# Loading q and k as long runs, in a softcap attention fused with a bilinear feed-forward layer

## The chip, the core and the metric

The kernel runs on one core of a Trainium2 chip. Time is device time of one launch in microseconds (us). The engines are TensorE (PE, with its weight loads as PEld), VectorE (DVE), ScalarE (ACT), GpSimd (POOL) and SyncE (SP); SP, ACT and POOL have queues from which they issue DMAs.

## The reference, cut to what matters

```python
# q, k, v: (4, 12, 448, 64) float32, cap a scalar; w_a, w_b: (768, 1536), w_out: (1536, 768), float64
scores = np.matmul(q, k.transpose(0, 1, 3, 2)) / np.sqrt(64)
scores = cap * np.tanh(scores / cap)
attn = softmax(scores)                       # over the keys, 1e-9 added to the sum
x = np.matmul(attn, v)                       # heads side by side: (1792, 768)
out = (x @ w_a) * (x @ w_b) @ w_out          # (1792, 768) float32
```

The weights come as 64-bit floats and are made into 32-bit floats on the chip, by integer operations on the two halves of each word (`load64`, `conv`).

## The kernel before, in words

**Pairs.** The 48 heads are worked through as 24 pairs. Pair `pi` has head `hp` on partitions 0 to 63 and head `hp + 6` on partitions 64 to 127. For each pair q and k are loaded (`load_k`), transposed to "feature by position" in 32 x 32 blocks on DVE (`turn`), and multiplied on PE (`scores`, four pieces `c`: three of 128 keys for both heads, one of the last 64). ACT makes tanh of each piece and exp of each half (`tanh`, `exp`); PE multiplies by v (`attend`, two halves); DVE adds the probabilities up and PE sums them (`add_full`, `add_last`, `sums_last`, `sums`). The reciprocal of the sums goes to DRAM and comes back spread over 64 partitions as `den` (`store_rec`, `load_den`); DVE scales (`scale`) and splits x into two parts, `xhi` and `xlo` (`split_x`).

**Two half batches.** Pairs 0 to 11 are the first half batch, and their x stays in SBUF. Pairs 12 to 23 are interleaved with the feed-forward layer of the first half (`hidden`, `gate`, `project`, `collect`), and their x is stored in DRAM for the second. `hidden(g, f, nm, h)` covers columns of x for batch `h` of the half: `h = 1` reads x of pairs 6 to 11. Each feed-forward product is made of three products of high and low parts.

**How q and k are loaded (lines 204 to 220).** One transfer `n` fills 32 partitions: `n` is a head of the pair and a half of its 64 features. It takes 32 features of each key, 128 bytes, so a head is 448 packets. Pairs 0 and 1 are loaded head by head, k from SP and q from ACT; pairs 2 to 11 two pairs at a time, from SP, into the accumulator `acc`, which nothing else uses yet; pairs 12 to 23 into one buffer for k and one for q (`ld`).

**The order of the work.** The order on every engine is written out once, when the program is built. PE's order is fixed by hand (`scores_of`, `attend_of`, `sums_of`, and `ffn(us)`, which puts in about `us` of feed-forward pieces). For the rest a planner (lines 513 to 848) gives each job an engine, a cost in us, a lag until its result can be used, and what it needs; due times run back from PE's order. It simulates the engines and, whenever one is free, picks the startable job that is due first. `MOVE` is a transfer's time in this model. Every engine then executes its list strictly in order. The order of SP's queue therefore also decides what a transfer waits behind.

**The start.** `warm_up` (lines 741 to 755) clears constants on DVE and runs dummy matmuls on PE. `load_cap` is issued by ACT after q of pair 0; `limits` computes six values from it on DVE, one exp on ACT, two more values on DVE, before the first tanh.

Of the kernel before, what the change touches and what calls it, by code (L numbers as in the profile page):

```python
# [119 lines left out]
def kernel(  # L120
# [75 lines left out]
    own, krem = (slice(0, D), slice(D, P)), (S - R, 0)  # L196
# [5 lines left out]
    early_rows = acc.rearrange("p t d -> p (t d)")  # L202

    def load_k(pi, nm, n, heads):
        b, hp = divmod(pi, NP)
        src = k if nm == "k" else q
        j, h = divmod(n, D // BLK)
        if pi < NPG:
            at = (NP * (nm == "q") + hp) * S
            if n == 0:  # L210
                for i in range(heads):
                    raw[nm, pi + i] = early_rows[:, at + i * S : at + (i + 1) * S]
            to = early_rows[n * BLK : (n + 1) * BLK, at : at + heads * S]
        else:
            if n == 0:
                raw[nm, pi] = ld.tile([P, S], F32, tag=f"ld{nm}", name=f"ld{nm}_{pi}")
            to = raw[nm, pi][n * BLK : (n + 1) * BLK]
        rows = src[b, j * NP + hp : j * NP + hp + heads].rearrange("m s d -> (m s) d")
        eng = nc.scalar if nm == "q" and pi < 2 else nc.sync
        eng.dma_start(to.rearrange("p (c d) -> p c d", d=BLK), rows[:, h * BLK : (h + 1) * BLK].rearrange("(c p) d -> p c d", p=BLK))  # L220

    def load_v(pi, n):
        b, hp = divmod(pi, NP)
        t = vb[pi % 3]
        j = n % 2
        src = v[b, hp + j * NP]
        eng = nc.gpsimd if 3 <= pi < NPG else nc.sync
        if n < 2:
            rows = src[j * R : j * R + NC3 * P].rearrange("(c p) d -> p c d", p=P)
            eng.dma_start(t[:, j * (NC3 + 2) : j * (NC3 + 2) + NC3], rows)  # L230
        else:
            eng.dma_start(t[own[j], NC3 + j], src[krem[j] : krem[j] + R])
# [18 lines left out]
    def last_keys(pi):  # L251
        for z, x in zip(kz, stk["k", pi]):
            for j, o in enumerate(own):
                nc.scalar.copy(z[o, j * R : (j + 1) * R], x[o, krem[j] : krem[j] + R])
# [3 lines left out]
    def scores(pi, c):  # L258
        tk, tq = stk["k", pi], stk["q", pi]
        psc = ps_sc.tile([P, 2, 512], F32, tag="pssc", name=f"psc_{pi}_{c}")  # L260
        full = c < NC3
        if pi < NPG:
            for j, o in enumerate(own):
                at = j * R + c * P if full else krem[j]
                to = psc[:, j, :S] if full else psc[o, 0, :S]
                nc.tensor.matmul(to, tk[o, at : at + (P if full else R)], tq[o], start=True, stop=True)  # L266
        elif full:
            for x, y in products:
                for j, o in enumerate(own):
                    kk = tk[x][o, j * R + c * P : j * R + (c + 1) * P]  # L270
# [253 lines left out]
    def loads(pi, heads):  # L524
        pairs = range(pi, pi + heads)
        for nm in "kq":
            eng = "ACT" if nm == "q" and pi < 2 else "SP"
            for n in range(P // BLK):
                free = [("turn", nm, p - NP) for p in pairs] if pi < NPG else [("turn", nm, pi - 1)]
                needs = [("load", nm, pi, n - 1)] if n else free  # L530
                job(("load", nm, pi, n), eng, 0.52, load_k, (pi, nm, n, heads), needs, 3.2 if pi < 2 else 4.0)
                jobs["load", nm, pi, n].order_only = n > 0
                for p in pairs:
                    jobs["load", nm, p, n] = jobs["load", nm, pi, n]
        for p in pairs:
            for n in range(4):
                eng, us = ("POOL", 0.7) if 3 <= p < NPG else ("SP", 0.52)
                needs = [("load", "v", p, n - 1)] if n else [("attend", p - 3, 1)]
                job(("load", "v", p, n), eng, us, load_v, (p, n), needs, 4.0)
                jobs["load", "v", p, n].order_only = n > 0  # L540
# [29 lines left out]
    def turns(pi):  # L570
        for nm in "kq":
            free = [("scores", pi - 2, c) for c in range(SUB)] + [("lo", nm, pi - 1)]
            job(("turn", nm, pi), "DVE", 0.56, turn, (pi, nm), [*(("load", nm, pi, n) for n in range(P // BLK)), *free])
# [21 lines left out]
    def attend_of(pi):  # L595
        for hf in range(2):
            on_pe(("attend", pi, hf), 1.52, attend, (pi, hf), [("exp", pi, hf), *evac.get(pv_bank(pi), ()), *(("load", "v", pi, n) for n in range(4))])
        if pi in ON_PE:
# [7 lines left out]
    def ffn_piece(key):  # L606
# [21 lines left out]
        else:  # L628
# [8 lines left out]
            if f == NF // GF - 1:  # L637
                if (g, x) == (NG - 1, NTI - 1) or h:
                    job(("out", g, x, h), "SP", 0.5, store_out, (g, x, h), [("collect", g, f, x, 0), ("collect", g, f, x, h)])
# [19 lines left out]
    SOON, RAW, BACKLOG = 4.0, 24.0, 3.0  # L659
# [3 lines left out]
    for pi, heads in ((0, 1), (1, 1), *((i, 2) for i in range(2, NPG, 2)), *((i, 1) for i in range(NPG, NPAIR))):  # L663
        loads(pi, heads)
# [3 lines left out]
    for pi in range(NPG):  # L668
        for c in (0, 1):
            scores_of(pi, c)  # L670
        if pi:
            attend_of(pi - 1)
# [13 lines left out]
    for pi in range(NPG, NPAIR + 1):  # L686
# [5 lines left out]
        if pi < NPAIR:  # L692
# [5 lines left out]
            ffn(GAP / 2 if pi > NPG else 7.2)  # L698
# [13 lines left out]
    for t, (nm, f, g) in enumerate(seq):  # L712
        if g == 0:
            parts = 6 if t < 4 else 2
            for n in range(parts):
                needs = [("raw", t, n - 1)] if n else [("conv", t - 2, 5)]
                job(("raw", t, n), "POOL" if t < 6 else "SP", 0.8 if t < 6 else 0.5, load64, (t, n, parts), needs, 4.0, RAW + 6.0 * (t + n / parts) if t < 4 else 0.0)
                jobs["raw", t, n].order_only = n > 0
            steps = (("ACT", 0.82), ("ACT", 0.8), ("DVE", 0.48), ("DVE", 0.48), ("DVE", 0.88), ("POOL", 2.1))
            for n, (eng, us) in enumerate(steps):  # L720
# [3 lines left out]
                job(("conv", t, n), eng, us, conv, (t, n), needs, 0.5)  # L724
# [15 lines left out]

    def warm_up():
# [7 lines left out]
        nc.vector.memset(sel, 0.0)  # L749
        for z in kz:  # L750
            nc.vector.memset(f32(z), 0.0)
        nc.vector.memset(sel[:, Q - QS : Q], 1.0)
        nc.vector.memset(both, 0.0)
        for j, o in enumerate(own):
            nc.vector.memset(both[o, Q + (j - 1) * QS : Q + j * QS], 1.0)

    def limits():
# [5 lines left out]
        nc.vector.tensor_scalar_mul(capt[:, 1:2], capt[:, 6:7], 1.0 / math.sqrt(D))  # L763
        nc.scalar.activation(capt[:, 7:8], capt[:, 0:1], AF.Exp, scale=-1.0)
# [3 lines left out]
    def load_cap():  # L768
        nc.scalar.dma_start(capt[:, 3:4], cap.rearrange("(a b) -> a b", b=1).to_broadcast([P, 1]))

    job("cap", "ACT", 0.5, load_cap, (), [("load", "q", 0, 3)], 2.4)
    jobs["cap"].order_only = True
    job("limits", "DVE", 1.3, limits, (), [("turn", "q", 0), "cap"])
    jobs["tanh", 0, 0].needs.append("limits")

# [35 lines left out]
    order, port, moved = [], 0.0, 0.0  # L811
    MOVE = {load_k: 0.46, load_v: 0.5, load64: 1.7, store_rec: 0.15, load_den: 0.4, store_w: 1.0, reload_w: 1.0, store_x: 0.57, reload_x: 0.65, store_out: 1.0}
    def starts(x):
# [3 lines left out]
        if x.move and x.fn not in (store_rec, load_den):  # L817
            t = max(t, moved - BACKLOG)
        return t

    for x in real:
        x.move = MOVE.get(x.fn, 0.0) * (x.args[3] if x.fn is load_k else 0.2 if x.fn is load_v and x.args[1] > 1 else 2 / x.args[2] if x.fn is load64 else 1.0)
        x.shared = x.eng == "DVE" and x.fn not in (turn, recip, scale, collect) and not (x.fn is gate and x.args[3] == 0)
    while len(order) < len(real):
# [12 lines left out]
        if x.move:  # L837
            moved = max(moved, t + 1.3) + x.move
            x.end = max(x.end, moved + 0.7)
# [54 lines left out]
```

## Time and profile before

| | us |
|---|---|
| median of 3 runs | 717.72 (717.03 to 718.0) |
| the profiled execution | 718.51 |
| its span | 716.7 |
| PE busy | 703.4 |
| DVE busy | 423.0 |
| ACT busy | 347.7 |
| POOL busy | 112.0 |

The span runs from the first to the last instruction; the execution's own time has 1.8 us around it. PE's busy time contains the dummy matmuls of the start. In rows of the trace "idle before" is the time that an engine stood still ahead of an instruction, and the arrow names what ended it. Times in rows count from the span's start.

### The profile page before, as it was taken

What the parts mean: (1) busy time and instruction counts of PE and PEld (TensorE: products, weight loads), DVE (VectorE), ACT (ScalarE), POOL (GpSimd) and SP (SyncE); (2) the same over time, 40 slices, a digit from 0 to 9 for tenths busy, and PEclk for the clock granted to TensorE, in tenths of its full rate; (3) what the DMA queues carried; (4) which work ended last, traced back from release to release, by engine and by line L of the source; (5) the groups of instructions that cost most, each with busy time, mean ns of one, the idle gap of its engine ahead of it and who ended that gap; (6) DMA issues with size and microseconds to landing.
All of it is one profiled execution on the core that took longest, in us unless ns stands there. A gap on an engine that the chain in (4) does not pass through costs nothing.

```text
span 716.7 us, 11238 instructions
## 1 busy us (share of the span) xinstructions
PE 703.4 (98%) x4370; PEld 578.3 (81%) x4370; DVE 423.0 (59%) x649; ACT 347.7 (49%) x474; POOL 112.0 (16%) x104
## 2 busy tenths in 40 slices
PE   7999998999999999999999999999999999999996
PEld 2333356879879789779879779999999999999996
DVE  4678897676679688686974849432043424434232
ACT  5989986577777566575646630222321112202100
POOL 0536431231322222222221100000000000000000
PEclk9999999999999999999999999999999999999999
DMA  9999585758777857858646437331022013101013
GB/s 128 152 171 170 140 212 123 193 143 200 184 170 193 193 141 177 201 138 227 157 116 159 146 101 248 110 109 45 11 83 83 23 34 99 53 15 44 1 45 113
DMA packets 142739, 90.55 MB, mean 126 GB/s; under 512 B 108024, under 2 KB 128536, under 8 KB 142680
## 3 DMA queue, kind: packets, MB, share of 16 engines
q1 hardware_dynamic: 135784, 82.53, 46.8%
q0 software_dynamic: 3040, 6.79, 4.0%
q10 hardware_dynamic: 3856, 0.46, 0.5%
q8 instruction: 36, 0.59, 0.4%
q14 instruction: 23, 0.19, 0.1%
HBM read 67.24 MB, written 22.50 MB: 125 GB/s over the span
## 4 chain that ended last, share of the span: by engine, by line
PE 92%; DMA 3%; SPq 2%; DVE 1%; ACT 1%; issue 0%; ACTq 0%; DVEq 0%
PE pv L308 10%; PE po L493 8%; PE po L494 8%; PE po L495 8%; PE phb L460 8%; PE phb L462 8%; PE phb L461 8%; PE pha L460 8%; PE pha L462 8%; PE pha L461 8%; PE psc L266 5%; PE psc L271 3%; DMA den<-rd 2%; PE pv L329 2%; SPq L220 1%; PE psc L274 1%
## 5 line engine op out<-in xcount | busy, mean ns | idle before, releaser
L493 PE MATMUL po<-who,gh 128*128 128x384 f32 x336 | 113.4, 337 | 0.0
L495 PE MATMUL po<-who,gl 128*128 128x384 f32 x336 | 112.5, 335 | 0.0
L494 PE MATMUL po<-wlo,gh 128*128 128x384 f32 x336 | 112.5, 335 | 0.0
L460 PE MATMUL pha<-xhi,wha 128*128 128x448 f32 x288 | 105.0, 365 | 2.7 <-DVE xhi L374 2.7
L460 PE MATMUL phb<-xhi,whb 128*128 128x448 f32 x288 | 105.2, 365 | 0.0
L462 PE MATMUL pha<-xhi,wla 128*128 128x448 f32 x288 | 104.8, 364 | 0.0
L461 PE MATMUL pha<-xlo,wha 128*128 128x448 f32 x288 | 104.6, 363 | 0.2 <-DVE xlo L375 0.2
L462 PE MATMUL phb<-xhi,wlb 128*128 128x448 f32 x288 | 104.6, 363 | 0.0
L461 PE MATMUL phb<-xlo,whb 128*128 128x448 f32 x288 | 104.3, 362 | 0.0
L283 ACT ACTIVATE pf<-psc,capt 128x896 f32<-128x896 f32 (+1 forms) x96 | 84.3, 909 | 29.6 <-PE psc L271 19.3
L308 PE MATMUL pv<-pf,vb 128*64 128x448 f32 x384 | 78.8, 553 | 0.0
L287 ACT ACTIVATE pf<-pf,capt 128x1792 f32<-128x1792 f32 (+1 forms) x48 | 77.1, 1606 | 0.8
L504 DVE TENSOR_TENSOR acc<-po,acc 128x384 f32<-128x384 f32 x84 | 46.4, 553 | 43.0 <-PE po L495 42.9
L467 ACT COPY asb<-pha 128x448 f32<-128x448 f32 x48 | 25.4, 531 | 81.8 <-PE pha L462 81.0
L493 PEld LDWEIGHTS po<-who,gh 128*128 128x128 f32 x336 | 63.1, 188 | 2.4 <-issue 1.2
L494 PEld LDWEIGHTS po<-wlo,gh 128*128 128x128 f32 x336 | 63.1, 188 | 0.1
L495 PEld LDWEIGHTS po<-who,gl 128*128 128x128 f32 x336 | 63.1, 188 | 0.0
L308 PEld LDWEIGHTS pv<-pf,vb 128*64 128x64 f32 x384 | 25.8, 139 | 45.5 <-issue 38.0
L477 DVE TENSOR_TENSOR asb<-phb,asb 128x448 f32<-128x448 f32 x48 | 29.9, 622 | 53.4 <-PE phb L462 53.4
L460 PEld LDWEIGHTS pha<-xhi,wha 128*128 128x128 f32 x288 | 54.0, 187 | 8.8 <-DVE xhi L374 3.4
L460 PEld LDWEIGHTS phb<-xhi,whb 128*128 128x128 f32 x288 | 54.0, 187 | 6.4 <-issue 2.5
L479 ACT CAST gh<-asb 128x448 fp32r<-128x448 f32 x48 | 27.2, 566 | 66.0 <-DVE asb L477 65.6
(103 smaller groups left out, 1038.4 us busy)
## 6 DMA issues: line engine op xcount, KB each, us to landing
w64o<-in_moe_w_out_dram SPq DMA_DIRECT2D x24, 384.0 KB
w64a<-in_moe_w_a_dram SPq DMA_DIRECT2D x18, 384.0 KB
w64b<-in_moe_w_b_dram SPq DMA_DIRECT2D x18, 384.0 KB
den<-rd SPq DMA_DIRECT2D x48, 112.0 KB
out_dram<-acc SPq DMA_DIRECT2D x13, 384.0 KB
wda<-wta SPq DMA_DIRECT2D x12, 384.0 KB
wdb<-wtb SPq DMA_DIRECT2D x12, 384.0 KB
wdo<-wto SPq DMA_DIRECT2D x12, 384.0 KB
```

The costliest lines, as they stand in the source:

```text
L266: nc.tensor.matmul(to, tk[o, at : at + (P if full else R)], tq[o], start=True, stop=True)
L283: nc.scalar.activation(to, prob.pop((pi, "s", c))[:, :n, :S], AF.Tanh, scale=capt[:, 1:2])
L287: nc.scalar.activation(pf, pf, AF.Exp, scale=capt[:, 0:1])
L308: nc.tensor.matmul(t[o, :S], tv[:, j * (NC3 + 1) + (c if j == 0 else (c + 1) % (NC3 + 1))], p, start=(c == 0), stop=(c == NC3))
L460: nc.tensor.matmul(t[:, :S], wh[:, kk], xhi[:, kk, cs], start=(kk == 0), stop=False)
L461: nc.tensor.matmul(t[:, :S], wh[:, kk], xlo[:, kk, cs], start=False, stop=False)
L462: nc.tensor.matmul(t[:, :S], wl[:, kk], xhi[:, kk, cs], start=False, stop=(kk == NK - 1))
L477: nc.vector.tensor_mul(t, phs.pop(("b", h))[:, :S], t)
L493: nc.tensor.matmul(t[:, :HALF], gh[:, cs], wh, start=(f == fs[0]), stop=False)
L494: nc.tensor.matmul(t[:, :HALF], gh[:, cs], wl, start=False, stop=False)
L495: nc.tensor.matmul(t[:, :HALF], gl[:, cs], wh, start=False, stop=(f == fs[-1]))
L504: nc.vector.tensor_add(acc[:, ti, hs], t, acc[:, ti, hs])
```

## The change

A transfer of q or k now takes, for each of 32 partitions, one run of consecutive memory: partition p gets keys 14 p to 14 p + 13, all 64 features of each but the last 32 of the last key (or the first 32 of the first). So each of the two transfers of a head brings also the features that it doesn't use, and 14 x 64 numbers a partition are kept where 14 x 32 are read. The transpose reads blocks of 32 features and writes with a stride of 14 elements, so that keys come out in their order. The remaining 64 keys (`rest`) are now the last ones for both heads, before they were the first ones for the second head.

With this go: each pair is loaded by itself (before, pairs 2 to 11 came two at a time); six slots in `acc` instead of twelve, so a load waits for the transpose of three pairs before; from pair 12 on one buffer for k and q together; pair 0 is loaded in turn from SP and ACT. Cap is loaded by POOL at the very start; `limits` is cut in two, and only the first part stands before the first tanh. Memsets move from DVE to POOL; the dummy matmuls are nine of 128 columns. Raw weights 4 and 5 move from POOL's queue to SP's. On PE the first half of `attend(0)` goes ahead of the scores of pair 1, and after the scores of pair 12 only 3.6 us of feed-forward are put in instead of 7.2. The planner's costs change, and it lets no more than 8 transfers be under way.

```diff
     def load_k(pi, nm, n):
...
-        rows = src[b, j * NP + hp : j * NP + hp + heads].rearrange("m s d -> (m s) d")
-        eng = nc.scalar if nm == "q" and pi < 2 else nc.sync
-        eng.dma_start(to.rearrange("p (c d) -> p c d", d=BLK), rows[:, h * BLK : (h + 1) * BLK].rearrange("(c p) d -> p c d", p=BLK))
+                at = (2 * pi + (nm == "q")) % EARLY * RUN
+                raw[nm, pi] = rows_of[:, at : at + RUN]
+            else:
+                raw[nm, pi] = ld.tile([P, RUN], F32, tag="ld", name=f"ld{nm}_{pi}")
+        width = RUN - D + BLK
+        eng = nc.scalar if pi == 0 and n % 2 else nc.sync
+        runs = src.rearrange("(p c) d -> p (c d)", p=BLK)
+        eng.dma_start(raw[nm, pi][n * BLK : (n + 1) * BLK, :width], runs[:, h * BLK : h * BLK + width])
...
     def turn(pi, nm):
-        t = raw.pop((nm, pi))
+        t = raw.pop((nm, pi)).rearrange("p (c d) -> p c d", d=D)[:, :, :BLK]
         tt = qk.tile([P, S], F32, tag=f"t{nm}", name=f"t{nm}_{pi}")
-        nc.vector.transpose(tt, t)
         stk[nm, pi] = tt
+        nc.vector.transpose(tt.rearrange("p (d c) -> p c d", d=BLK), t)
...
-        eng = nc.gpsimd if t < 6 else nc.sync
+        eng = nc.gpsimd if t < 4 else nc.sync
...
+            free = [("turn", nm, pi - EARLY // 2)] if pi < NPG else [("turn", "q", pi - 1)] if nm == "k" else [("turn", "k", pi)]
...
+        if pi == 1:
+            attend_of(0, (0,))
...
-            ffn(GAP / 2 if pi > NPG else 7.2)
+            ffn(GAP / 2 if pi > NPG else 3.6)
...
     def warm_up():
+        load_cap()
         warm = bank(0, "warm")
-        nc.vector.memset(psum[0][:, 0], 0.0)
-        for n in (S, S, S, S // 2):
-            nc.tensor.matmul(warm[:, :n], psum[0][:, 0, :P], psum[0][:, 0, :n], start=True, stop=True)
+        nc.vector.memset(psum[0][:, 0, :P], 0.0)
+        for n in range(9):
+            nc.tensor.matmul(warm[:, :P], psum[0][:, 0, :P], psum[0][:, 0, :P], start=True, stop=True)
...
+    job("limits", "DVE", 1.0, limits, (), (), None, 4.0)
+    job("floors", "DVE", 0.4, floors, (), ["limits"])
+    for c in range(2):
+        jobs["tanh", 0, c].needs.append("floors" if c else "limits")
```

## Rows read from the trace of the kernel before

**Rows 1.** The page, part 1: busy time, share and instructions by engine.
```profile
PE 703.4 (98%) x4370; PEld 578.3 (81%) x4370; DVE 423.0 (59%) x649; ACT 347.7 (49%) x474; POOL 112.0 (16%) x104
```

**Rows 2.** Table by stretch, PE alone: stretch, length, busy, clock, DMA share, GB/s.
```profile
0.00:20.00 20.00, 15.92 (x58) 1.00 0.96 132
...
80.00:130.00 50.00, 47.04 (x418) 0.97 0.68 150
...
440.00:716.70 276.70, 270.77 (x1430) 1.00 0.20 64
```

**Rows 3.** Instructions in order of time, 0 to 30 us: start, duration, instruction.
```profile
0.75 4.32 SPq L220 DMA_DIRECT2D acc<-in_k_dram  x7
...
1.40 5.05 PE L745 MATMUL warm<-psum 128*128 128x448 f32 x8 [1.40 <-DVE psum L743]
...
6.11 0.65 DVE L237 STREAM_TRANSPOSE tq<-acc 128x448 f32<-128x448 f32 x1 [3.11 <-DMA capt<-in_cap_dram]
...
7.14 1.28 ACT L764 ACT_TABLE_LOAD   x1 [7.14 <-DMA acc<-in_q_dram]
...
7.33 1.77 PE L266 MATMUL psc<-tq,tk 64*128 64x448 f32 x8 [0.89 <-DVE capt L758]
...
7.99 0.15 DVE L763 TENSOR_SCALAR capt<-capt 128x1 f32<-128x1 f32 x1
...
8.54 1.89 ACT L283 ACTIVATE pf<-psc,capt 128x896 f32<-128x896 f32 x2
...
12.82 1.92 PE L266 MATMUL psc<-tq,tk 64*128 64x448 f32 x8 [1.32 <-ACT pf L283]
```

**Rows 4.** Chain of waits, 0 to 20 us: start, duration, what.
```profile
12.25 0.53 ACT pf L283
```

**Rows 5.** Chain of waits, 80 to 130 us.
```profile
95.37 2.25 DMA den<-rd
...
109.24 0.42 SPq L220
...
112.90 5.98 DMA den<-rd
...
121.62 0.60 PE pha L461
```

**Rows 6.** Waits of PE: us in total, times, longest.
```profile
PE pha L460 <- DVE xhi L374: 2.7, 1, 2.7
```

**Rows 7.** Table by stretch, PE alone, after the wait at 118.
```profile
120.96:127.60 6.64, 6.45 (x49) 0.74 0.23 37
```

**Rows 8.** DMA view, 0 to 2 us (rate in 40 slices) and 2 to 4 us.
```profile
GB/s 0 0 0 0 0 0 0 0 0 0 0 0 0 0 0 0 0 0 0 0 0 0 0 0 0 0 0 0 0 0 0 0 0 0 0 10 72 84 105 95
...
DMA packets 2848, 0.35 MB, mean 176 GB/s; under 512 B 2848, under 2 KB 2848, under 8 KB 2848
```

**Rows 9.** Table by stretch, all engines; the last two columns are DMA share and GB/s.
```profile
500.00:600.00 100.00, 100.00 (x531) 96.13 (x530) 32.00 (x47) 22.47 (x38) 0.00 (x0) 1.00 0.17 52
```

**Rows 10.** Groups of DVE instructions: shapes, count, busy us, mean ns, idle before.
```profile
L417 DVE SCALAR_TENSOR_TENSOR wta<-w64a,wta 128x768 int32<-128x768 int32 x12 | 11.3, 946 | 0.2
...
L237 DVE STREAM_TRANSPOSE tk<-ldk 128x448 f32<-128x448 f32 x12 | 7.6, 635 | 0.1
```

**Rows 11.** The page, part 6: DMA issues, KB each, median us to landing.
```profile
vb<-in_v_dram POOLq DMA_DIRECT2D x18, 16.0 KB, 3.7
```

**Rows 12.** Instructions in order of time, ACT and DVE, 95 to 130 us.
```profile
113.07 1.43 ACT L287 ACTIVATE pf<-pf,capt 128x1344 f32<-128x1344 f32 x1
...
119.52 1.08 DVE L294 TENSOR_TENSOR psum<-psum,pf 128x896 f32<-128x896 f32 x1
```

**Rows 13.** Table by stretch: busy PE, PEld, DVE, ACT, POOL; clock, DMA share, GB/s.
```profile
80.00:110.00 30.00, 29.91 (x313) 16.47 (x312) 27.42 (x46) 27.01 (x34) 9.63 (x12) 1.00 0.74 170
200.00:300.00 100.00, 100.00 (x638) 83.56 (x637) 77.95 (x109) 65.49 (x94) 23.14 (x12) 1.00 0.73 181
```

**Rows 14.** Waits of SP's DMA queue: us in total, times, longest.
```profile
SPq L220 <- DVE tk L237: 43.6, 9, 7.2
```

More of the change, by code (lines that the diff above doesn't have):

```diff
@@ L194, with load_k @@
     vb = [const.tile([P, 2 * NC3 + 2, D], F32, tag=f"vb{i}", name=f"vb{i}") for i in range(3)]
-    own, krem = (slice(0, D), slice(D, P)), (S - R, 0)
+    own, rest = (slice(0, D), slice(D, P)), slice(S - R, S)
     raw, stk, prob, pvs = {}, {}, {}, {}
     ON_PE = set(range(3, NPG))
-    early_rows = acc.rearrange("p t d -> p (t d)")
-    def load_k(pi, nm, n, heads):
+    rows_of = acc.rearrange("p t d -> p (t d)")
+    RUN = S * D // BLK
+    EARLY = NTI * DM // RUN
+    def load_k(pi, nm, n):
         b, hp = divmod(pi, NP)
-        src = k if nm == "k" else q
         j, h = divmod(n, D // BLK)
[L208 to L217, printed above, removed]
-        rows = src[b, j * NP + hp : j * NP + hp + heads].rearrange("m s d -> (m s) d")
-        eng = nc.scalar if nm == "q" and pi < 2 else nc.sync
-        eng.dma_start(to.rearrange("p (c d) -> p c d", d=BLK), rows[:, h * BLK : (h + 1) * BLK].rearrange("(c p) d -> p c d", p=BLK))
+        src = (k if nm == "k" else q)[b, j * NP + hp]
+        if (nm, pi) not in raw:
+            if pi < NPG:
+                at = (2 * pi + (nm == "q")) % EARLY * RUN
[6 more added lines that the diff above has]
+        eng.dma_start(raw[nm, pi][n * BLK : (n + 1) * BLK, :width], runs[:, h * BLK : h * BLK + width])
     def load_v(pi, n):
@@ L263, in scores @@
             for j, o in enumerate(own):
-                at = j * R + c * P if full else krem[j]
                 to = psc[:, j, :S] if full else psc[o, 0, :S]
-                nc.tensor.matmul(to, tk[o, at : at + (P if full else R)], tq[o], start=True, stop=True)
+                kk = tk[o, c * P : (c + 1) * P] if full else tk[o, rest]
+                nc.tensor.matmul(to, kk, tq[o], start=True, stop=True)
         elif full:
@@ L522, in job, with loads @@
         jobs[key] = Piece(eng, us, LAG[eng] if lag is None else lag, list(needs), fn, args, after)
-    def loads(pi, heads):
-        pairs = range(pi, pi + heads)
+    def loads(pi):
         for nm in "kq":
-            eng = "ACT" if nm == "q" and pi < 2 else "SP"
+            free = [("turn", nm, pi - EARLY // 2)] if pi < NPG else [("turn", "q", pi - 1)] if nm == "k" else [("turn", "k", pi)]
             for n in range(P // BLK):
[L529 to L540, printed above, removed]
+                needs = free if n == 0 or pi == 0 else [("load", nm, pi, n - 1)]
+                job(("load", nm, pi, n), "ACT" if pi == 0 and n % 2 else "SP", 0.52, load_k, (pi, nm, n), needs, 3.0 if pi < 2 else 4.0)
+                jobs["load", nm, pi, n].order_only = n > 0 and pi > 0
+        for n in range(4):
+            eng, us = ("POOL", 0.7) if 3 <= pi < NPG else ("SP", 0.52)
+            needs = [("load", "v", pi, n - 1)] if n else [("attend", pi - 3, 1)]
+            job(("load", "v", pi, n), eng, us, load_v, (pi, n), needs, 4.0)
+            jobs["load", "v", pi, n].order_only = n > 0
     def softmax(pi):
@@ L572, in turns @@
             free = [("scores", pi - 2, c) for c in range(SUB)] + [("lo", nm, pi - 1)]
-            job(("turn", nm, pi), "DVE", 0.56, turn, (pi, nm), [*(("load", nm, pi, n) for n in range(P // BLK)), *free])
+            free += [("load", nm, pi, n) for n in range(P // BLK)]
+            job(("turn", nm, pi), "DVE", 0.56, turn, (pi, nm), free)
             if pi >= NPG:
@@ L593, in scores_of, with attend_of @@
         slots.append(("tanh", pi, c))
[L595 to L598, printed above, removed]
+    def attend_of(pi, halves=(0, 1)):
+        for hf in halves:
+            on_pe(("attend", pi, hf), 1.52, attend, (pi, hf), [("exp", pi, hf), *(() if hf else evac.get(pv_bank(pi), ())), *(("load", "v", pi, n) for n in range(4))])
+        if pi in ON_PE and 1 in halves:
             on_pe(("sums_last", pi), 0.35, sums_last, (pi,))
@@ L658 @@
     CYCLE, turns_of = ((0, 1, 2), (3, 1, 2, 0)), [3, 3, 1, 2, None]
-    SOON, RAW, BACKLOG = 4.0, 24.0, 3.0
+    SOON, RAW, BACKLOG, DEPTH = 4.0, 24.0, 3.0, 8
     HASTY = (gate, keep_a, collect, recip, store_rec, load_den, scale)
     GAP = 20.4
-    for pi, heads in ((0, 1), (1, 1), *((i, 2) for i in range(2, NPG, 2)), *((i, 1) for i in range(NPG, NPAIR))):
-        loads(pi, heads)
+    for pi in range(NPAIR):
+        loads(pi)
     for pi in range(NPAIR):
@@ L671 @@
         if pi:
-            attend_of(pi - 1)
+            attend_of(pi - 1, (0, 1) if pi > 1 else (1,))
         for c in (3, 2):
@@ L716 @@
                 needs = [("raw", t, n - 1)] if n else [("conv", t - 2, 5)]
-                job(("raw", t, n), "POOL" if t < 6 else "SP", 0.8 if t < 6 else 0.5, load64, (t, n, parts), needs, 4.0, RAW + 6.0 * (t + n / parts) if t < 4 else 0.0)
+                job(("raw", t, n), "POOL" if t < 4 else "SP", 0.8 if t < 4 else 0.5, load64, (t, n, parts), needs, 4.0, RAW + 6.0 * (t + n / parts) if t < 4 else 0.0)
                 jobs["raw", t, n].order_only = n > 0
@@ L723 @@
                     needs += [("lo", t - AHEAD), ("keepw", t - AHEAD), ("full", t - 1)]
-                job(("conv", t, n), eng, us, conv, (t, n), needs, 0.5)
+                job(("conv", t, n), eng, us, conv, (t, n), needs, 1.5 if eng == "POOL" else 0.5)
             job(("keepw", t), "SP", 0.52, store_w, (t,), [("conv", t, 5)], 3.0)
@@ L818, in starts @@
             t = max(t, moved - BACKLOG)
+        if x.move and x.eng != "POOL" and len(landed) >= DEPTH:
+            t = max(t, landed[-DEPTH])
         return t
     for x in real:
-        x.move = MOVE.get(x.fn, 0.0) * (x.args[3] if x.fn is load_k else 0.2 if x.fn is load_v and x.args[1] > 1 else 2 / x.args[2] if x.fn is load64 else 1.0)
-        x.shared = x.eng == "DVE" and x.fn not in (turn, recip, scale, collect) and not (x.fn is gate and x.args[3] == 0)
+        x.move = MOVE.get(x.fn, 0.0) * (0.2 if x.fn is load_v and x.args[1] > 1 else 2 / x.args[2] if x.fn is load64 else 1.0)
+        x.shared = x.eng == "DVE" and x.fn not in (turn, limits, floors, recip, scale, collect) and not (x.fn is gate and x.args[3] == 0)
     while len(order) < len(real):
@@ L838 @@
             moved = max(moved, t + 1.3) + x.move
-            x.end = max(x.end, moved + 0.7)
+            x.end = max(x.end, moved + (1.7 if x.fn is load64 else 0.7))
+            if x.eng != "POOL":
+                landed.append(t + x.us + 1.7 if moved < t + 1.6 + x.move else moved + 0.4)
         free[e] = t + x.us
```

33 lines of the change are left out of this document (15 added, 18 removed).

## The prediction

> **What bounds the kernel now.** I read the page first. TensorE (PE) is busy 703.4 of 716.7 us, and that is 98% of the span [rows 1]. So the whole kernel is a line of matmuls, and a change can win only where that line has holes. The table by stretch says where they are [rows 2]: 4.1 us in the first 20 us, 3.0 between 80 and 130, and the 5.9 of the last stretch, most of them the tail after the last matmul, which nothing here touches; of the 13.3 that the span has in all, 0.3 are left for everything else. The first 20 us hide more than 4.1, because 5.05 us of their busy time is the warm-up loop, which computes nothing [rows 3].
>
> Then I read both holes closely. At the start [rows 3]: q and k of pair 0 are transposed from 6.11 to 7.27, scores start at 7.33, the first tanh at 8.54, the first exp ends at 12.25, and from 12.82 PE runs without a hole of a microsecond. Up to there it does two rows of scores, 1.77 + 1.92 = 3.7 us of work. The chain of waits says what is late [rows 4]: ACT (ScalarE) is on it from 7.14, first with the table load, which stands behind ACT's own nine DMA issues [rows 3], then with tanh and exp up to 12.78.
>
> The second hole is the join of attention and feed-forward, at 118. The hidden piece with h = 1 needs x of pair 11. Its denominator was issued at 112.90 and took 5.98 us to land; scale, add and split follow, PE goes on with x's high part at 120.96 and with the low part at 121.62 [rows 5]. PE waits 2.7 us there [rows 6], and pays again: from 120.96 to 127.60 the granted clock averages 0.74, so part of that stretch ran at the lower level (1.2 GHz) after the wait. That is 0.26 x 6.64 = 1.7 us [rows 7]. The hole costs 4.4 us.
>
> **The change, part by part.**
>
> *Loads of q and k.* One transfer was 448 packets of 128 B (56 KB); it becomes 32 runs of 3456 B (108 KB), half of it thrown away. Between 2 and 4 us small packets moved at 176 GB/s with the engines full [rows 8]. Later, with rows of 3 KB, 52 GB/s were moved at a busy share of 0.17, so 306 at full share [rows 9]. Pair 0 is 8 transfers: 0.46 MB / 176 = 2.6 us before, 0.88 MB / 306 = 2.9 us after. So the bytes take no less time; the gain is in the order: all eight are now issued first, four from SP and four from ACT, while before three of k of pair 1 were already on their way by 5.07 and shared the engines [rows 3]. First bytes flow at 1.8 (the slices of that view are 0.05 us), 1.8 + 2.9 = 4.7, plus half a microsecond for v's transfers issued behind them: q is there at about 5.2, k before it. If the new runs went only at the 176 of the small ones, 5.0 us, it would be 7.3; that is the bad end.
>
> *Transpose.* 48 of them at some 635 ns for 448 elements a partition [rows 10]. Its write now has a stride of 56 B. No row shows such a write; the nearest is conv, which reads 768 elements at a stride of 8 B in 946 ns, 1.23 ns an element against the 1.42 of the transpose [rows 10]. By that row: no cost. The other bound is twice the time, +0.62 us each; gain I exclude, the elements are the same. I take 0.
>
> The Trainium skill (SBUF — State Buffer, section Door 1) says that SBUF is read and written in 16-byte lines and that a pattern that leaves its line with every access pays for it; 56 B does. No run here shows it; by it the transposes slow, which is the second rival below.
>
> *Cap first, limits split.* Cap goes from ACT's queue to GpSimd's (POOL) ahead of everything. A small POOL transfer lands 3.7 us after issue [rows 11], so at some 4.3; six small VectorE (DVE) operations (from 7.20, the last from 7.99 [rows 3]) then end by 5.2, before q's transpose. ACT has four issues instead of nine, so its table load (1.28 us, from 7.14 before) runs before 5. Scores can start at 5.2 + 0.65 (transpose, k's is done) + 0.1 = 5.95. The first scores take about 0.9 of the 1.77, so tanh starts near 6.95 instead of 8.54.
>
> *First half of attend(0) ahead of scores of pair 1.* Before, PE waited for the third tanh (12.78, that is 4.24 after the first); now it can start attend(0, 0) when exp ends, 3.71 after the first tanh [rows 3, 4]. PE's unbroken work begins at 6.95 + 3.75 = 10.70 instead of 12.82, with the same 3.7 us done before it: **-2.1 us**. Behind it, scores of pair 1 want their loads by 12: 16 issues from SP (pair 0 four, v four, pair 1 eight) at some 0.5 us (0.42 and the gap behind it [rows 5]) end by 9.5 and land by 11.7. That is covered, by half a microsecond.
>
> *Warm-up.* 9 x 128 = 1152 columns instead of 1568: 5.05 x 0.73 = 3.7 us from about 1.1, so it ends at 4.8 and the gap to scores is 1.15 (0.89 before). A gap of 1.32 before 12.82 left the granted clock at 1.00 [rows 2, 3]. I take no cost; were the clock low, the first scores cost some 0.9 us more. Bounds for the start as a whole: -3.2 (q at 4.2) to +0.6 (176 GB/s).
>
> *More issues.* Pairs 2 to 11 had 40 double transfers, now 80: +40 x 0.5 = 20 us of SP between 10 and 80, or 2 us per pair of 7.6 us (scores 2 x 1.9, attend 3.2, sums 0.6); the 8 issues take 4.2, with rec, den and weights some 6.5 in all. That is hidden by PE, which is the bound there. The rest of a pair (v, den) is unchanged, and the transfers have 3 pairs (23 us) ahead of need instead of 6. Raw weights 4 and 5 move from POOL to SP: 4 issues, 2 us, hidden likewise.
>
> *The join.* In place of 7.2 us of hidden pieces after the scores of pair 12 only 3.6 are put there, so attend(12) (3.2), sums (0.6) and the first scores of pair 13 (1.4) come ahead of the piece that waited. That moves its need of x of pair 11 from 118.1 to 123.3; x was ready at 121.6, so 1.7 us to spare without any faster DMA. Besides, between rec's store and the issue of den six loads of k and q were issued, 3.1 us, and their small packets lay ahead of den [rows 5]; a den on a quiet queue took 2.25. attend(12) wants its exp, which ended at 114.5 against 114.9: just there [rows 12]. So the hole goes with its clock loss: **-4.4 us** (bounds: 0, if another wait stands there, to -4.6).
>
> After 130 PE has no hole, DVE and ACT are busy 0.78 and 0.65 of 200 to 300 [rows 13], and the k and q pair has one shared buffer for 28 us of work per pair. I cost it at nothing; the cover is that slack.
>
> Sum on the profiled execution: 718.51 - 2.1 - 4.4 = **712.0 us**. The median of the runs shown is 0.8 lower than that execution; I leave 712.0, as the start term has more below it than above.
>
> **Rivals.**
>
> *The wait changes its place.* sums(12) needs the second add of pair 12. Before, it stood on DVE behind the scale that waited for den, and ended at 120.6 [rows 12]. If the written order keeps it there, PE waits at 118.1 for up to 2.5 us and loses the clock again (1.7): the join gives 0.3 to 1. For it: DVE is 0.91 busy from 80 to 110 [rows 13], and POOL, SP and DVE are all re-ordered by the planner. Against: sums is due earlier now, and the planner sorts by that. 718.5 - 2.1 - 0.5 = 715.9.
>
> *The stride is paid.* +0.62 us per transpose. At the start +0.6. From 80 to 110 six transposes, 3.7 us, meet 2.6 us of idle DVE [rows 13], so 1.1 to 3.7 late, say 2.4: 718.5 - 1.5 - 4.4 + 2.4 = 715.0. Elsewhere DVE has room.
>
> *Slower: the one buffer holds up SP.* From pair 12 on, q's load waits for k's transpose, and the next k's for q's; SP issues in order, so den, rec and the weights stand behind. SP already waits for tk 43.6 us, 4.8 each time [rows 14]. If two such waits stand ahead of rec and den of pair 11, x is 9.7 late, 8.0 beyond the 1.7 to spare; with the clock 9.7: 718.5 - 6.5 + 9.7 = 721.7. It turns to slower from 6.5 us of such waits (1.7 to spare and 1.7 of clock cancel out). Against: only k and q of pairs 12 to 14 fall before the join.
>
> *No gain at the start* (transfers at 176 GB/s) together with a moved wait: 718.5 + 0.1 - 0.5 = 718.1.
>
> **How the numbers follow.** Forecast 0.50, moved wait 0.20, stride paid 0.12, SP held up 0.12, nothing gained 0.06. A measurement of this kernel tells about 0.2% from no change, that is 716.3 and 719.2. Faster: 0.50 + 0.12 + 0.14 of the moved wait = 0.76. Same: 0.06 of it + 0.05 = 0.11. Slower: 0.13. The range 709.0 to 717.0 holds the first three (start at -3.2 and some of the 20 to 80 holes below, a moved wait at its worst above) and leaves out 0.18.
>
> **What would show it.** In the trace after: scores from about 6, first tanh near 7, PE without holes from about 10.7; attend(12) directly after the third hidden piece, no hole before the x split, granted clock 1.00 from 110 to 130; transposes at 0.62 us; 128-byte packets of q and k gone, about 6000 long ones in their place. Wrong if: transposes take 1.2 us; SP shows waits on tk or tq ahead of den; PE waits at sums(12) or scores of pair 13; ACT or DVE are late for the weights between 85 and 110 now that PE comes 2 us sooner.

## The result, and the profile after

The change makes the kernel slower: 728.23 us (four runs, 726.93 to 729.52) against 717.86 (717.03 to 719.6) in the same job, a ratio of 1.0141 with a 95% interval of 1.0113 to 1.0169. The profiled execution of after took 728.93 us with a span of 727.2; that is 10.5 more than the span of before.

The page of after, part 1 (busy us, share of the span, instructions), answers to [rows 1].

```profile
PE 707.0 (97%) x4380; PEld 580.5 (80%) x4380; DVE 436.0 (60%) x642; ACT 348.0 (48%) x474; POOL 110.2 (15%) x108
```

PE is busy 3.6 us longer with slightly less to compute and idle 6.9 us longer (20.2 against 13.3). The table of PE by stretch says where; it answers to [rows 2] (stretch, its length, PE busy, granted clock, DMA share, GB/s).

```profile
0.00:20.00 20.00, 14.99 (x58) 1.00 0.80 185
20.00:80.00 60.00, 57.69 (x508) 1.00 1.00 219
80.00:130.00 50.00, 44.77 (x385) 0.93 0.75 190
440.00:727.20 287.20, 281.50 (x1491) 0.99 0.22 70
```

Between 20 and 80 the DMA engines are full (share 1.00), and the large hole is new: it stands just before 83, where before had none. The last stretch idles 5.7 us, as before. PE's own list of waits (total, times, longest) answers to [rows 6].

```profile
PE psc L265 <- DVE capt L769: 3.6, 1, 3.6
PE pv L307 <- DVE den L357: 3.5, 1, 3.5
PE pv L307 <- ACT w64b L405: 2.2, 1, 2.2
PE pv L328 <- DVE psum L293: 1.8, 1, 1.8
```

The work is the same in both kernels, so I lay the two traces side by side by a landmark: the sums of a pair, 28 matmuls of 128x64. Sums of pair 0 start at 29.19 (26.82 before), so **the start costs 2.4 us**. Sums of pair 7 start at 91.26 (80.20 before); at sums of pairs 9 and 10 the difference is 10.9 (106.88 against 95.96). So 8.5 us come **behind the start**: 2 of them in small steps (1.6 between the sums at 51.93 and at 61.18) and 6.5 at the hole, between the sums at 77.13 and at 91.26. At the end it is 10.5: **the join gives back less than half a microsecond**.

*The start.* The timeline of after from 0 to 30, all engines (start, length, engine, line, operation, count, idle time before and what ended it), answers to [rows 3].

```profile
1.27 0.68 POOL L739 DMA_DIRECT2D capt<-in_cap_dram  x1 [0.80 <-POOLq L880]
...
5.94 0.15 DVE L759 TENSOR_SCALAR capt<-capt 128x1 f32<-128x1 f32 x1 [3.92 <-DMA capt<-in_cap_dram]
...
6.95 0.94 DVE L237 STREAM_TRANSPOSE tk<-acc 128x448 f32<-128x448 f32 x1
...
7.90 0.94 DVE L237 STREAM_TRANSPOSE tq<-acc 128x448 f32<-128x448 f32 x1
...
8.90 5.97 PE L265 MATMUL psc<-tq,tk 64*128 64x448 f32 x16 [3.62 <-DVE capt L769]
...
29.19 0.65 PE L328 MATMUL pv<-psum,sel 128*32 128x64 f32 x28
```

Cap lands 4.6 us after POOL's issue, at 5.9, and the six limits (5.94 to 6.95) now stand on DVE ahead of both transposes. q lands at 7.7, by the chain of waits (start, length, what):

```profile
2.16 5.55 DMA acc<-in_q_dram
```

So scores start at 8.90 instead of the 5.95 that I forecast, after 3.6 us in which PE does nothing. Sixteen instructions of scores then take 5.97 us, where before two rows of eight took 1.77 and 1.92 [rows 3]. The granted clock of 1.00 in the table is no reading here: the trace of after has no record of that clock before 13.77 us, and a stretch without a record counts as 1.00. The kernel with upper and lower partitions in turn (below) starts in nearly the same way and has records: after a wait of 3.48 us its clock stood at the lower level (1.2 GHz) from 8.68 to 12.09, and twelve scores took 4.25 us. So it is likely, and not shown, that the first scores of after ran at the lower level too.

*The hole.* The chain of waits from 41 to 90 (start, length, what) is almost all transfers, each wait an issue on SP's queue; it answers to [rows 5], whose chain ran through den as well but only at the join.

```profile
58.65 4.71 DMA acc<-in_k_dram
63.38 5.75 DMA acc<-in_q_dram
69.14 4.69 DMA acc<-in_q_dram
73.85 5.22 DMA acc<-in_k_dram
79.13 6.87 DMA rd<-rec
```

From 58.65 to 79.13 each step is a load of q or k that SP issued, and the next step is the eighth issue behind it on SP's queue, which begins 0.02 us after the first has landed (0.07 the last time). So SP, which issues in order, moves at the pace of landing: 4.7 to 5.8 us from one step to the next. The trace also says what waits there. SP's transfers tell of their landing on eight semaphores in turn, and each of these four issues waits for the semaphore that it will use itself, which the transfer eight places earlier still holds. So the wait stands in the program, in before as well, and is not one that the chip imposes.

Rec and den stand in this line. The den that is late for the hole is that of pair 4. Its reciprocal on DVE, the store of rec and the loads of den, in after and then in before (from the timelines of DVE and SP):

```profile
65.70 0.55 DVE L336 RECIPROCAL rec<-rec 112x64 f32<-112x64 f32 x1
...
70.55 0.79 SPq L340 DMA_DIRECT2D rd<-rec  x1
...
74.79 1.12 SPq L350 DMA_DIRECT2D den<-rd  x2
```
```profile
58.54 0.55 DVE L337 RECIPROCAL rec<-rec 112x64 f32<-112x64 f32 x1
...
59.32 0.80 SPq L341 DMA_DIRECT2D rd<-rec  x1
...
64.04 1.11 SPq L351 DMA_DIRECT2D den<-rd  x2
```

From the end of the reciprocal to the store's issue it takes 4.3 us (0.2 before), from there to the first load of den 4.2 (4.7), and den has landed at 82.3, 7.5 later (at 67.5, 3.5 later). That is 16.1 us against 8.4: 4 us more in SP's line, and 4 more for den's own transfers while the engines are full. The last steps on the way to PE stand in the timelines of DVE and of PE:

```profile
82.33 0.63 DVE L357 TENSOR_TENSOR den<-pv,den 128x448 f32<-128x448 f32 x1 [5.25 <-DMA den<-rd]
```

```profile
77.13 0.65 PE L328 MATMUL pv<-psum,sel 128*32 128x64 f32 x28
...
83.01 6.11 PE L307 MATMUL pv<-pf,vb 128*64 128x448 f32 x16 [3.46 <-DVE den L357]
```

DVE stands 5.25 us at the scale that wants den. PE's next attend needs the accumulator that this scale reads, and waits 3.46. It pays twice, like the join of before: the 16 instructions of attend take 6.11 us instead of 3.23, at a granted clock of 0.52, that is nearly all at the lower level (1.2 GHz). By PE's table:

```profile
83.01:89.05 6.04, 6.04 (x16) 0.52 0.43 155
```

What comes next is late by this: the reciprocal of the sums at 77.13 stands behind that scale in DVE's order and starts at 87.10, 10 us after its sums. DVE's waits for den (total, times, longest) add up to 21.7 us; before it was the second row.

```profile
DVE den L357 <- DMA den<-rd: 21.7, 12, 5.2
```
```profile
DVE den L358 <- DMA den<-rd: 5.8, 8, 3.1
```

### The profile page after: what moved, and what is told of

Its sections match the earlier page's. It is cut to its first block, busy times and chain, and to the rows that moved or that the text cites. A ratio compares the mean times of both kernels' runs of the same rounds, so it can differ in the third digit from the quotient of the medians.

```text
span 727.2 us, 11329 instructions
## 1 busy us (share of the span) xinstructions
PE 707.0 (97%) x4380; PEld 580.5 (80%) x4380; DVE 436.0 (60%) x642; ACT 348.0 (48%) x474; POOL 110.2 (15%) x108
## 4 chain that ended last, share of the span: by engine, by line
PE 73%; DMA 14%; DVE 5%; SPq 4%; issue 1%; ACT 1%; POOL 0%; ACTq 0%; DVEq 0%
PE po L492 8%; PE po L494 8%; PE po L493 8%; PE phb L459 7%; PE phb L461 7%; PE phb L460 7%; PE pha L459 7%; PE pha L461 7%; PE pha L460 7%; PE pv L307 4%; DMA acc<-in_q_dram 3%; PE psc L270 3%; DMA rd<-rec 2%; DMA w64o<-in_moe_w_out_dram 2%; SPq L219 2%; DMA den<-rd 2%
## 5 line engine op out<-in xcount | busy, mean ns | idle before, releaser
L307 PE MATMUL pv<-pf,vb 128*64 128x448 f32 x384 | 80.6, 562 | 6.0 <-DVE den L357 3.5
```

The lines of the kernel that those rows point to most:

```text
L307: nc.tensor.matmul(t[o, :S], tv[:, j * (NC3 + 1) + (c if j == 0 else (c + 1) % (NC3 + 1))], p, start=(c == 0), stop=(c == NC3))
```

## The experiments

My theory (BYTES): the doubled bytes of q and k fill the DMA engines, SP's queue runs at the pace of landing, and rec and den, in that queue, come late. Rivals: STRIDE (slower transposes hold up DVE), QUEUE (the number of SP's issues, whatever they carry), and START (the late start and its clock). The expectations also name ORDER: the new order on every engine and the shallower buffers cost the time, whatever is loaded.

### Contiguous write of the transpose: is it the stride?

```diff
-nc.vector.transpose(tt.rearrange("p (d c) -> p c d", d=BLK), t)
+nc.vector.transpose(tt.rearrange("p (c d) -> p c d", d=BLK), t)
```

> The changed kernel (728.2 us) with the transposes writing contiguously, so that keys come out in another order (the result is not the reference's); everything else, the order on every engine too, is that of the change. In the changed kernel a transpose took 0.93 to 0.99 us instead of 0.62 to 0.64. Theory BYTES (the longer transfers fill the DMA engines, and rec and den wait behind them): transposes fall to about 0.62 us, the time hardly, 725 to 728. Theory STRIDE (48 x 0.31 = 15 us more on DVE is what is late): 718 to 721. Theory ORDER (the re-planned order and the shallower buffers cost it, whatever is loaded): 727 to 728.

729.23 us, ratio to before 1.0146 [1.0118, 1.0174]: no gain. The transposes did get faster. DVE's groups (count, busy us, mean ns, idle before and its end), of after and then of this kernel:

```profile
L237 DVE STREAM_TRANSPOSE tk<-ldk 128x448 f32<-128x448 f32 x12 | 11.9, 988 | 0.5 <-DMA ldk<-in_k_dram 0.3
```
```profile
L237 DVE STREAM_TRANSPOSE tk<-ldk 128x448 f32<-128x448 f32 x12 | 7.7, 640 | 0.7 <-DMA ldk<-in_k_dram 0.6
```

988 against 640 ns, and the time stands where it was: the stride is real and costs nothing here. STRIDE falls.

### Half the bytes, same issues, same order

```diff
+eng.dma_start(raw[nm, pi][n*BLK:(n+1)*BLK, :S], runs[:, h*S:(h+1)*S])
+t = raw.pop((nm, pi))[:, :S].rearrange("p (c d) -> p c d", d=BLK)
```

> The changed kernel with each q and k transfer cut to runs of 1792 B (32 runs, 56 KB, so half of the numbers that the transposes read are wrong ones and the result is not the reference's); number and place of the transfers as in the change. BYTES: the 5 us wait of DVE for den at 77 and PE's 3.5 us hole behind it go, 714 to 720. STRIDE: 726 to 728. ORDER: 726 to 728.

717.22 us, 0.9979 [0.9963, 0.9996]: the whole loss is gone with 32 runs of 1792 B in place of 3456, and PE has no hole at 80. The store of rec of pair 4 is issued 0.7 us after the end of its reciprocal, in the same order in which it took 4.3 in after. QUEUE falls in its simple form, since the number and the order of issues are those of after, and ORDER falls as a cause by itself for the same reason. Whether the full bytes would cost anything with deeper buffers is not tested here.

### Small packets of before, one pair per transfer

```diff
+eng.dma_start(to, src.rearrange("(p c) d -> p c d", p=BLK)[:, :, h*BLK:(h+1)*BLK])
```

> The changed kernel with only the wanted 32 features of each key loaded, 448 packets of 128 B a transfer (56 KB) into the same slots, same order on all engines. BYTES in the sense of data moved: 716 to 722, nearly as x2. If packets count as much as bytes (the engines were as full before with 128 B packets at 0.93 share to 100 us): 724 to 730, and x2 alone is fast. STRIDE: 727 to 728. ORDER: 727 to 729.

739.19 us, 1.0303 [1.0281, 1.0325], the slowest of all. I had taken the bytes to be all there is, and they are not: an issue of 448 short packets holds SP itself longer. The DMA issues by line (least, median, most ns of one; from, to; count), here and in after:

```profile
L218 SPq DMA_DIRECT2D acc<-in_k_dram x46: 567/621/841, 0.8 to 85.6; - x46
```
```profile
L219 SPq DMA_DIRECT2D acc<-in_k_dram x46: 310/419/1424, 0.8 to 76.0; - x46
```

0.62 against 0.42 us; the chain of waits of this kernel from 30 to 90 is SP's own issuing of q and k for 28.3%. So the long runs do save something, 0.2 us of SP each, and SP's line can be bound by issue as well as by landing.

### The join alone, on the kernel before

```diff
-ffn(GAP / 2 if pi > NPG else 7.2)
+ffn(GAP / 2 if pi > NPG else 3.6)
```

> The kernel before (717.9 us) with one edit of the change alone: 3.6 us of feed-forward instead of 7.2 after the scores of pair 12. My step on the join: the 2.7 us hole at 118 and its 1.7 us at the low clock go, 713.5. Rival (the wait moves to sums(12) or to attend(12)): 716 to 718.

716.63 us, 0.9971 [0.9949, 0.9994]. The wait moved, as my first rival said, to sums, and costs 1.1 us there instead of 2.7. PE's timeline:

```profile
119.40 0.65 PE L329 MATMUL pv<-psum,sel 128*32 128x64 f32 x28 [1.14 <-DVE psum L294]
```

Its table has the clock at 1.00 throughout, so the second payment is saved:

```profile
100.00:140.00 40.00, 38.86 (x269) 1.00 0.78 184
```

### rec and den on POOL's queue, and q on POOL's queue

```diff
-nc.sync.dma_start(rd[pi]...)      # and likewise den
+(nc.gpsimd if pi < NPG else nc.sync).dma_start(rd[pi]...)
```

> The changed kernel with rec's store and den's two loads of pairs 0 to 11 issued from POOL's queue instead of SP's, at the same place of the order. In the chain of the changed kernel SP issues a transfer 0.02 us after the one eight issues before has landed, in steps of 4.7 to 6.9 us, and rec and den stand in that line. Theory QUEUE (what is late is the small transfers' place in SP's line behind bulk loads): rec to scale falls to about 7 us, PE's holes between 40 and 90 go, 716 to 721. Theory ENGINES (the 16 engines are full, share 1.06 from 60 to 80, so every transfer is late whatever its queue): 725 to 730.

735.41 us, 1.0246 [1.02, 1.0292]. It tells nothing apart: POOL issues in order too, so its raw weights and v now wait for rec, and they lead the chain of waits from 30 to 90 instead (weights 21.4%, v 12.3%).

```diff
+eng = nc.scalar if pi == 0 and n % 2 else nc.gpsimd if nm == "q" and 0 < pi < NPG else nc.sync
```

> The changed kernel with q's loads of pairs 1 to 11 issued from POOL's queue at the same place of the order, so half of the bulk stands in another line. QUEUE: SP's line is half as long, 716 to 722. ENGINES: the same bytes on the same engines, 725 to 730. If POOL's own work (its issues at 0.54 us, v, raw weights, conv) becomes late: over 730.

729.79 us, 1.0165 [1.0122, 1.0209]. Half of the early loads are off SP's queue and the time is that of after; the DMA engines are as full (share 1.00 from 40 to 60, 216 GB/s). But it is lost in another place. DVE's waits for den fall from 21.7 to 10.8 us, so the shorter line on SP does help den, and PE waits for it nowhere. Now q is late: it stands on POOL's queue behind raw weights, and DVE and then PE wait for it:

```profile
50.80 0.97 DVE L237 STREAM_TRANSPOSE tq<-acc 128x448 f32<-128x448 f32 x1 [4.32 <-DMA acc<-in_q_dram]
```
```profile
58.41 3.56 PE L265 MATMUL psc<-tq,tk 64*128 64x448 f32 x8 [3.52 <-ACT pf L282]
```

So neither run tells whether rec and den would be in time on a queue that carries no bulk at all.

### Twice the warm-up

```diff
-for n in range(9):
+for n in range(18):
```

> The changed kernel with 18 dummy matmuls instead of 9, so that PE has no hole of 3.6 us before its first scores. The first scores took 5.97 us for 16 instructions where 8 took 1.77 in the kernel before. If the low clock there is on the path: 726.5 to 727.3 (first tanh and all behind it about 1 us sooner). If what comes later (den) sets the time: no difference, 728.

728.13 us, 1.0134 [1.0091, 1.0176]. The start does improve; the timeline of the kernel:

```profile
1.07 6.00 PE L746 MATMUL warm<-psum 128*128 128x128 f32 x36 [1.07 <-DVE psum L744]
...
8.66 1.77 PE L265 MATMUL psc<-tq,tk 64*128 64x448 f32 x8 [1.59 <-DVE capt L769]
...
27.52 0.65 PE L328 MATMUL pv<-psum,sel 128*32 128x64 f32 x28
```

Eight scores take 1.77 us again, and sums of pair 0 come 1.7 earlier than in after. By the sums that after has at 77.13 PE is 2.6 later than after (79.73): whatever PE gains early it waits for again. START falls as the cause of the loss, and the 2.4 us at the start are no term that can be added to the end.

### Single loads on the kernel before

```diff
-for pi, heads in ((0, 1), (1, 1), *((i, 2) for i in range(2, NPG, 2)), *((i, 1) ...)):
+for pi, heads in ((i, 1) for i in range(NPAIR)):
```

> The kernel before with one edit: the loads of pairs 2 to 11 one pair at a time (80 transfers of 448 packets instead of 40 of 896), 12 slots as before. In x3 an issue of 448 packets took SP 0.62 us and SP's issues made up 28% of the chain. If the number of issues is what the small packets cost: SP late, 722 to 732. If x3 was slow because of the six slots and the order: 717 to 720.

721.88 us, 1.0036 [1.0015, 1.0058]: twice the issues of short packets without any more bytes cost 2.4 us (721.88 against 719.5 in the same job). That is just below the 722 to 732 that I had expected if the number of issues counts. An issue takes 0.48 us here (median of 48).

### Upper and lower partitions in turn

```diff
+m, n = n, (0, 2, 1, 3)[n]
```

> The changed kernel with the four transfers of a q or k in the order partitions 0-31, 64-95, 32-63, 96-127 instead of 0-31, 32-63, 64-95, 96-127. Between 8 and 14 us the changed kernel moved 228 GB/s at a busy share of 0.89, 256 at full share, where I had taken 306 from rows on 128 partitions. If the long runs are slow because neighbouring transfers write the same half of the partitions: over 280 at full share and 718 to 724. If the engines simply need the time per byte: the same rate, 726 to 730.

725.48 us, 1.0105 [1.0074, 1.0136]. The tables of 8 to 14 us (stretch, its length, then busy PE, PEld, DVE, ACT, POOL, granted clock, DMA share, GB/s), of after and of this kernel:

```profile
8.00:14.00 6.00, 5.10 (x14) 1.63 (x16) 2.60 (x5) 2.67 (x3) 0.00 (x0) 1.00 0.89 228
```
```profile
8.00:14.00 6.00, 5.03 (x16) 1.68 (x16) 2.49 (x5) 2.81 (x3) 0.00 (x0) 0.72 0.84 236
```

At full share that is 256 and 281 GB/s. The Trainium skill (SBUF — State Buffer, Door 1) says that a transfer into 32 partitions reaches only 8 of SBUF's 16 ports, and that partitions 0 to 63 share one half of them. The rates agree with it in direction. From 40 to 80, in mixed traffic, the two kernels move the same (216 and 227 GB/s in the two halves of that stretch in after, 224 and 223 here), and the intervals of the two times overlap, so this stays open. (The granted clock of 0.72 holds the stretch at the lower level; the 1.00 of after is no reading before 13.77.)

### The stride alone, on the kernel before

> The kernel before with one edit: the transpose writes with the stride of the change (keys come out in another order, so the result is not the reference's). Transposes go from 0.62 to about 0.95 us, 15 us more of DVE in all. If that has cover: 717.5 to 719.5. If it is late where DVE is full (80 to 110): 719.5 to 722.

719.46 us, 1.0016 [0.9995, 1.0037]. (The edit is the written pattern of after in the transposes of before.) The transposes take 980 ns and DVE is busy 27.78 of the 30 us from 80 to 110:

```profile
80.00:110.00 30.00, 29.76 (x324) 15.34 (x323) 27.78 (x47) 26.84 (x33) 10.77 (x14) 1.00 0.74 174
```

PE has 0.24 us of holes there: DVE's slack holds it, as long as den is in time.

### The dose: how the time goes with the bytes

```diff
+width = 672        # and 864; the half-bytes kernel has 448
+eng.dma_start(raw[nm, pi][n*BLK:(n+1)*BLK, :width], runs[:, :width])
```

> As x2 (the transposes read the first 448 numbers of a partition, so the result is not the reference's), but each run brings 2688 B instead of 1792; the rest is never read. BYTES: between x2 (717.2) and the changed kernel (728.2), 719 to 725, the share of the DMA engines from 40 to 80 between theirs (0.70 and 1.03). If what x2 changed was the place that the transposes read: as x2, 716 to 718.

> As x2 and x12, but each run brings 3456 B as in the change; half of it is never read. BYTES: as the changed kernel, 726 to 730, although nothing uses the added bytes. If what x2 changed was the place that the transposes read: as x2, 716 to 718.

722.14 us, 1.0040 [1.0025, 1.0055], and 727.68 us, 1.0110 [1.0088, 1.0132]. With runs of 1792, 2688 and 3456 B the ratios are 0.9979, 1.0040 and 1.0110; none of the intervals overlap. The table of 40 to 80 us shows what fills up (columns as above), for 1792, 2688, 3456 B unread and after:

```profile
40.00:80.00 40.00, 39.78 (x388) 14.86 (x384) 37.59 (x58) 38.87 (x40) 27.88 (x37) 1.00 0.70 188
```
```profile
40.00:80.00 40.00, 39.56 (x376) 14.81 (x374) 34.22 (x50) 38.30 (x39) 25.45 (x36) 1.00 0.86 220
```
```profile
40.00:80.00 40.00, 37.91 (x366) 14.20 (x362) 31.40 (x45) 38.16 (x39) 25.04 (x35) 1.00 1.00 217
```
```profile
40.00:80.00 40.00, 37.91 (x366) 14.07 (x362) 31.85 (x46) 37.53 (x38) 25.89 (x35) 1.00 1.02 222
```

DMA share 0.70, 0.86, 1.00, 1.02: full at 3456 B, and there PE falls behind (37.91). DVE's wait for den follows it, 12.3, 16.2, 22.2 and 21.7 us:

```profile
DVE den L356 <- DMA den<-rd: 12.3, 7, 4.3
```
```profile
DVE den L357 <- DMA den<-rd: 16.2, 8, 4.4
```
```profile
DVE den L357 <- DMA den<-rd: 22.2, 10, 6.1
```

The issues, their order, the transposes and the join are the same in all three, so it is the length of the runs, and with it the bytes, that sets the loss. BYTES stands. The way from den to PE is seen at full length alone: PE itself waits for den 5.7 us at 3456 B unread and 3.5 in after, but 0.2 at 2688 B. There its holes of 1.3 and 0.6 us stand at 83 to 86, behind tanh on ACT, and the attend behind them takes 4.52 us instead of 3.23.

### A version from the parts that hold

On the kernel before: the join with 3.6, the first half of attend(0) ahead of scores of pair 1, cap from POOL, limits and floors left to be placed by the planner so that they fall behind the transposes.

> The kernel before with three edits of the change that load nothing more: 3.6 us of feed-forward at the join, the first half of attend(0) ahead of the scores of pair 1, and cap from POOL first with limits cut in two (after q's and k's transposes on DVE). x4, the first edit alone, was 0.3% faster than before. If the start's edits give what I had taken without the loads (0.5 from attend, 0.3 from the first tanh): 0.4% faster than before, some 715 to 716. If nothing at the start reaches the end: as x4, 0.3%.

715.71 us, 0.9967 [0.995, 0.9985]: faster than both kernels, by 0.33% (2.4 us) than before. Sums of pair 0 start at 26.34 (26.82 before), so the start gives 0.5 us; the rest is the join, whose wait at sums is 1.4 us here. The join alone (0.9971) can't be told from it.

## Why the prediction was wrong

I said 712.0, with 709 to 717; it is 728.2. Of the 16.9 us that the profiled execution is over the forecast, 4.5 lie at the start (+2.4 for -2.1), 8.5 between start and join (forecast 0), and 4.0 at the join (-0.4 for -4.4). Step by step:

- **Loads of q and k: "52 GB/s were moved at a busy share of 0.17, so 306 at full share ... 0.88 MB / 306 = 2.9 us after. So the bytes take no less time."** This is the step that failed. I took the rate from transfers of other shape, in a stretch in which the DMA engines stood at a share of 0.17. Measured at 8 to 14 us: 228 GB/s at a share of 0.89, 256 at full. Worse, I applied it to pair 0 alone and never asked for the 10 to 80 us behind it, where the table of before already shows little room:

```profile
40.00:80.00 40.00, 40.00 (x378) 15.27 (x378) 31.39 (x49) 36.66 (x36) 24.58 (x38) 1.00 0.88 167
```

  The share was 0.88. From 20 to 40 it was higher still:

```profile
20.00:40.00 20.00, 19.70 (x160) 7.17 (x158) 13.39 (x20) 18.67 (x17) 8.53 (x15) 1.00 1.19 160
```

  PE is busy 19.70 of those 20 us, so full engines alone did not hold it up; the loads of before stood six pairs ahead of their need, those of after three. The DMA queues of 40 to 80 (packets, MB, share of 16 engines), before and after, give the size:

```profile
q1 hardware_dynamic: 15829, 3.51, 54.6%
```
```profile
q1 hardware_dynamic: 2801, 5.73, 66.5%
```

  The queue of SP's transfers went from 3.51 to 5.73 MB, its time from 21.8 to 26.6 of 40 us. A byte got cheaper (161 to 215 GB/s at full share), but not twice as cheap, and half of the bytes of q and k are thrown away. At 306 the 5.73 MB would have been 18.7 us, and the change would have relieved the engines.
- **More issues: "hidden by PE, which is the bound there."** I counted what SP issues (0.5 us each), and the issues were about that (0.42). What I left out is that an issue waits for a landing, and that den's own transfer takes longer in full engines (7.5 us for 3.5). The price of this step was put at 0; with the bytes of the step above, which are its cause, it is 8.5 us. My row for it stood there: a den took 5.98 us to land at 112.90 [rows 5], so the pace of landing was a measured thing.
- **Start: -2.1, bounds -3.2 to +0.6.** It is +2.4 to the sums of pair 0. q lands at 7.7 and not 5.2, later even than the bad end of 7.3; cap at 5.9 and not 4.3, limits and two slow transposes stand in a row on DVE, and PE's gap before scores is 3.6 us and not 1.15. "I take no cost" for that gap was wrong as well: 16 scores in 5.97 us, 8 in 1.77 with a longer warm-up. The bounds moved q alone; cap and limits, which stand ahead of q's transpose on DVE, had none. The bound for 176 GB/s is also written in two ways, +0.6 here and +0.1 in the last rival; by the chain itself, q at 7.3 for 5.2, it is 0.0.
- **Join: -4.4.** Alone it is -2.3 (716.63 against 718.91 in the same job), by the moved wait that I had as a rival at 715.9. The rival had the place right and the price too high: it took the clock as lost again, and there it was not. In after there are 2.2 and 1.8 us of waits in that place, for the weights on ACT and the second add, by PE's timeline; late weights were among the signs that I named:

```profile
114.00 3.23 PE L307 MATMUL pv<-pf,vb 128*64 128x448 f32 x16 [2.22 <-ACT w64b L405]
...
133.41 0.65 PE L328 MATMUL pv<-psum,sel 128*32 128x64 f32 x28 [1.78 <-DVE psum L293]
```

- **Transpose: 0, bounds 0 to +0.62.** It is +0.35, half way, and costs nothing on the path. The Trainium skill (SBUF — State Buffer, Door 1) has a pattern that leaves its 16-byte line with every access pay; the trace agrees (988 against 640 ns), and the time does not show it.
- **The slower rival** had the right queue and the wrong place. SP held up by the one buffer from pair 12 on did not come: its wait for tk is 42.3 us, 43.6 before [rows 14]. SP was held up by landing, before pair 12.

Open: how much of the loss is SP's line and how much den's own slow landing. At the hole they are some 4 us each, but no run takes one away and leaves the other: a kernel in which SP's issues wait for no earlier landing, or in which rec and den have a queue of their own, was not tried.

## What to carry to other kernels

Before a change adds bytes to a queue, read the DMA share of the stretch in which they move, not of the stretch where the rate looks best: at a share of 0.88, a load that moves twice the bytes in longer packets wins only if a byte gets more than twice as cheap. Read with it how far ahead of their need the loads stand: at 1.19 the kernel before lost nothing. A small transfer that PE's order depends on (here rec and den) is at risk in the queue that carries the bulk. That moving it helps is not shown: the two runs that used POOL's queue instead lost the time there. When a part of a change looks good by itself, run it by itself: the join was worth 2.3 us, and the loads cost nearly four times that.

## What was not expected of the hardware

- With the engines full, the two loads of a den (112 KB each, the first issued at 74.79) took 7.5 us until both had landed, against 3.5 in before (64.04).
- After 3.6 us without work at the start, scores took 5.97 us for sixteen instructions, in a stretch for which the trace has no record of the clock until 13.77; with the longer warm-up and a gap of 1.59, eight took 1.77.
- Loads of 3456 B runs into 32 partitions: 256 GB/s at full share (228 at 0.89) from 8 to 14, 217 to 222 in mixed traffic, against the 306 of the rows of 3 KB [rows 9].
- A transposing write at a stride of 56 B costs 0.98 instead of 0.64 us for 448 numbers a partition, while a read of 768 numbers at a stride of 8 B cost 0.946 [rows 10].
- SP takes 0.42 us to issue 32 long runs, 0.48 for 448 packets of 128 B in the order of before and 0.62 for as many in the order of the run.
- A transfer of one number to each of 128 partitions from POOL landed 4.6 us after its issue began.
